# One 512-column moving operand for two groups of tokens in the first product of a retention and MLP kernel

## The chip, the cores and the metric

One core of one Trainium2 chip. The metric is the device time of one execution, in microseconds, as a median of runs. Engines are called as in the profile: PE is TensorE, DVE is VectorE, ACT is ScalarE, POOL is GpSimd, SP is SyncE.

## The reference

Two parts, one behind the other, all in float32 (B 4, H 8, S 768, D 64; 3072 tokens, d_model 512, d_ff 2048):

```python
for t in range(S):                       # retention, for each batch and head
    state = gamma * state + k[t] (outer) v[t]
    y[t] = scale * q[t] @ state
x = y as [3072 tokens, 512]
h = x @ w_in                             # the first product
g = h * erf(softplus(h))                 # the gate
out = g @ w_out                          # the second product
```

`w_in` and `w_out` arrive in 64-bit words and are converted in the kernel.

## The kernel before

**Tiling.** The 3072 tokens are 24 chunks of 128 and 12 groups of 256 (`GT`), two chunks to a group. d_ff is 16 pieces of 128 (`ft`), or 8 pairs of them (`n`). Both products run on operands that are split into rounded rows: each float32 operand becomes `hi`, `lo` and `dif` in float32r, and three matmuls stand for one. `hi` and `lo` products add up in one PSUM bank `a`, `dif` in another, `b`; `together` (lines 284 and 285) puts them together, ScalarE first, VectorE second.

**First stage.** Groups 0 and 1 are done in a prologue with float32 matmuls (line 620) while `w_in` is being converted. From group 2 on there is one period for each group g. It holds eight units; `unit(g, n)` makes two pieces of d_ff for the 256 tokens of g with 24 matmuls of 256 columns (line 645), and its `put` evacuates them into a tile `h` and writes `h` to DRAM (`HID`, line 668, GpSimd's queue). Units take turns at two pairs of PSUM banks; in the last period at four pairs.

Into the periods, in an order written out by hand, go:

- on TensorE, `on_pe`: the retention for the next group's chunks a = 2g+2 and b = 2g+3. `begin` (lines 526 and 533: scores from k and q, then k times v) stands before the unit with index 2, `results` (lines 571 and 582) before the one with index 5;
- on ScalarE and VectorE, `beside`: `states`, `crossed_sums` (line 601) and `split_x` (lines 276 to 278), which makes the next group's split rows `x_hi`, `x_lo`, `x_dif`; `prepare`, which transposes the next k and q (line 505), scales q (line 500) and, at the start of the following period, scales v (line 510); the conversion of `w_out` (`convert`), which ends in a write of float32 rows to DRAM (`WOF`, line 238); splits of weights (lines 268 to 270);
- on SyncE's queue, `load_pair`: 32 small loads of k and q (line 144), two of v (line 133), two of k (line 155) for the chunks after next;
- on GpSimd's queue, `load_quarter`: the loads of `w_out` (line 187), one in each unit of the first period and then in units 2 to 5.

The order of the program is kept on each engine. Tiles of 4 KB for each partition come from one pool of 39 slots (`big`), of 8 KB from a pool of 4 (`wide`: `w_in` and `w_out` as they arrive, later the first split pieces of `w_out`). A slot is handed on when the last access to its tile is over, and the first writer of the new tile waits for that.

**Second stage.** For each group and quarter of d_ff, a load of 512 KB from `HID` (line 763), softplus (768), erf (772), product (782), split (276 to 278), and 24 matmuls of 512 columns (line 827). The first groups' gates and the splits of `w_out` are begun in the last two periods of the first stage.

Of the kernel before, what the change touches and what calls it, by code (L numbers as in the profile page):

```python
# [21 lines left out]
P = 128  # L22
# [27 lines left out]
def kernel(  # L50
# [21 lines left out]
    n_ft = d_ff // P  # L72
    NPC = n_ft // 2
    DH = d_model // 2
    assert D == 64 and d_model == H * D and n_k == HP == 4 and S % GT == 0 and NJ % 2 == 0
    assert H == 8 and n_ft == 16 and NC > JPC and GT == 2 * C

    const = ctx.enter_context(tc.tile_pool(name="const", bufs=1))
    big = ctx.enter_context(tc.tile_pool(name="big", bufs=39))
    small = ctx.enter_context(tc.tile_pool(name="small", bufs=6))  # L80
    wide = ctx.enter_context(tc.tile_pool(name="wide", bufs=4))
    scratch = ctx.enter_context(tc.tile_pool(name="scratch", bufs=1, space=bass.MemoryType.DRAM))
    ps_r = ctx.enter_context(tc.tile_pool(name="ps_r", bufs=2, space=PSUM))
    ps_h = ctx.enter_context(tc.tile_pool(name="ps_h", bufs=2, space=PSUM))
# [10 lines left out]
        return wide.tile([P] + shape, dtype, name=name, tag="b8")  # L95


    HID = [scratch.tile([P, n_ft, GT], F32, name=f"hid{g}") for g in range(NG)]
    WOF = [scratch.tile([P, 2, d_model], F32, name=f"wof{n}") for n in range(NPC)]

    KN, QN, V, KB, QB, KT, QT, SC, AM, SU = {}, {}, {}, {}, {}, {}, {}, {}, {}, {}
# [65 lines left out]
    def load_piece(n, part=None):  # L167

        if n not in RAW:
            RAW[n] = b8("raw", [2 * d_model], I64)  # L170
        f = slice(2 * P) if part is None else slice(part * P, (part + 1) * P)
        each = 1 if part is None else 2
        for g in range(0, n_k, each):
            nc.sync.dma_start(
                RAW[n].rearrange("p (g f) -> p g f", g=n_k)[:, g : g + each, f],
                w_in[g * P : (g + each) * P, n * 2 * P : (n + 1) * 2 * P].rearrange(
                    "(g p) f -> p g f", p=P
                )[:, :, f],
            )
# [13 lines left out]
    def conversion(n):  # L193

        WF[n] = b4("w", [2, 2, 2 * P])
        POWER[n] = b4("power", [2, 2, 2 * P])
        for part in range(2) if n < 4 else (None,):
            f = slice(2 * P) if part is None else slice(part * P, (part + 1) * P)  # L200
            words = RAW[n].bitcast(U32).rearrange("p (h a b w) -> p h a b w", h=2, a=2, w=2)[:, :, :, f]
            to, power = WF[n][..., f], POWER[n][..., f].bitcast(U32)
            number = to.bitcast(U32)
            lo, hi = words[..., 0], words[..., 1]
            nc.vector.tensor_scalar(power, hi, 0x7FF00000, None, op0=ALU.bitwise_and)
            exponent = partial(nc.scalar.activation, power, power, AF.Relu, bias=below, scale=8.0)
            if n < NPC:
                exponent()
            else:
                behind.append(exponent)  # L210
            yield
            nc.vector.tensor_scalar(
                number, hi, 0xFFFFF, 1 << 20, op0=ALU.bitwise_and, op1=ALU.bitwise_or
            )
            if part is None:
                yield
            nc.vector.scalar_tensor_tensor(to, number, 2.0**32, lo, op0=ALU.mult, op1=ALU.add)
            yield
            nc.vector.scalar_tensor_tensor(
                power, hi, 1 << 31, power, op0=ALU.bitwise_and, op1=ALU.bitwise_or  # L220
            )
            if part != 0:
                del RAW[n]
                if n + 4 < NPC:
                    load_piece(n + 4)
                if n < 2:
                    load(JPC + n)
                    load_values(JPC + n)
            if part is None:
                yield  # L230
            nc.vector.scalar_tensor_tensor(
                to, to, 2.0**-52, power.bitcast(F32), op0=ALU.mult, op1=ALU.mult,
            )
            if n < NPC:
                done.update(("in", 2 * n + u) for u in (range(2) if part is None else (part,)))
            yield
        if n >= NPC:
            nc.gpsimd.dma_start(
                WOF[n - NPC], WF.pop(n).rearrange("p h a f -> p (h a f)").rearrange("p (f c) -> p f c", f=2)
            )  # L240

    def weights():

# [359 lines left out]
    def split_x(j):  # L603
        g, i = divmod(j, 2)
        if i == 0:
            X[g] = [b4(f"x_{x}", [HP, GT], F32R) for x in ("hi", "lo", "dif")]
        at = slice(i * C, (i + 1) * C)
        split(X[g], (slice(None), slice(None), at), XC[g][:, :, at])

# [25 lines left out]
    def unit(g, n):  # L635
# [26 lines left out]
        def put():  # L662
# [3 lines left out]
            else:  # L666
                together(h, a, b)
            nc.gpsimd.dma_start(HID[g][:, 2 * n : 2 * n + 2], h)  # L668

        return put  # L670

# [86 lines left out]
    def load_hidden(n):  # L758
# [1 line left out]
        if n >= NG * NU:  # L760
            return
        HID_[n] = b4("hid", [4, GT])
        nc.sync.dma_start(HID_[n], HID[n // NU][:, n % NU * 4 : n % NU * 4 + 4])

    def softplus(k):
        for n in (2 * k, 2 * k + 1) if k < NH else ():
# [26 lines left out]
        nc.sync.dma_start(WO[n], WOF[n])  # L793

    first_w = []

    def split_w_out(n):
        to = None
        if n < 2:
            if n == 0:  # L800
                first_w.extend(b8(f"w_{x}", [2, 2 * d_model], F32R) for x in ("hi", "lo", "dif"))
            to = [x[:, n] for x in first_w]
        if n == 2:
            x = b8("w_2", [2, 2 * d_model], F32R)
            to = [x[:, 0], x[:, 1], b4("w_dif", [2 * d_model], F32R)]
        split_weights(n, WO.pop(n), to, W_OUT)

    Y = {}
# [35 lines left out]
        for n in (2 * k, 2 * k + 1):  # L844
            load_hidden(n)

    def on_pe(g):

        a, b = 2 * g + 2, 2 * g + 3
        if a >= NJ:  # L850
            return {}
        if g < NG - 2:
            m = 3 if g == G2 else 2
            return {
                m: [(begin, a, ps_h), (begin, b, ps_r)],
                5: [(results, a, None, ps_h), (results, b, None, ps_r)],
            }
        return {1: [(begin, a)], 2: [(results, a)], 3: [(begin, b)], 5: [(results, b)]}

    def beside(g, prep, next_prep):  # L860

        a, b = 2 * g + 2, 2 * g + 3
        if g == G2:
            return {
                1: [(split_weights, 4)],
                2: [(split_weights, 5)],
                3: [(states, a), (states, b)],
# [1 line left out]
                5: [(crossed_sums, a), (split_x, a)],  # L869
                6: [(crossed_sums, b), (split_x, b)],  # L870
                7: [(steps, next_prep, 3)],
            }
        if g == G2 + 1:
            return {
                0: [(steps, prep)],
                1: [(split_weights, 7)],
                2: [(states, a)],
                3: [(states, b)],
                5: [(crossed_sums, a), (split_x, a)],
                6: [(crossed_sums, b), (split_x, b)],  # L880
                7: [(steps, next_prep, 3)],
            }
        if g < NG - 2:
            return {
                0: [(steps, prep)] + [(convert, 1)] * (g < NG - 3),
                1: [(convert, 2)],
                2: [(states, a), (convert, 1)],
                3: [(states, b), (convert, 1)],
                4: [(convert, 2)],
                5: [(crossed_sums, a), (split_x, a)],  # L890
                6: [(crossed_sums, b), (split_x, b)],
                7: [(steps, next_prep, 3)],
            }
        if g == NG - 2:
            return {
                0: [(steps, prep), (load_w_out, 0)],
                1: [(states, a), (load_w_out, 1)],
                2: [(crossed_sums, a), (split_w_out, 0), (load_hiddens, 0)],
                3: [(states, b), (split_x, a)],
                4: [(split_w_out, 1), (softplus, 0)],  # L900
                5: [(erf, 0), (crossed_sums, b), (load_w_out, 2)],
                6: [(split_x, b), (gated, 0), (load_hiddens, 1)],
                7: [(split_w_out, 2), (split_g, 0)],
            }
        return {
            0: [(split_g, 1), (softplus, 1), (load_w_out, 3)],
            1: [(erf, 1), (load_w_out, 4)],
            2: [(split_w_out, 3), (load_w_out, 5)],
            3: [(gated, 1), (split_w_out, 4)],
            4: [(split_g, 2), (load_w_out, 6), (load_hiddens, 2)],  # L910
            5: [(split_w_out, 5), (load_w_out, 7)],
            6: [(split_g, 3)],
            7: [(split_w_out, 6)],
        }

    for g in range(G2, NG):
        pair = load_pair(2 * g + 4) if 2 * g + 4 < NJ else iter(())
        next_prep = prepare(2 * g + 4) if 2 * g + 4 < NJ else iter(())
        pe, other = on_pe(g), beside(g, prep, next_prep)
        for i, n in enumerate((0, 7, 1, 2, 3, 4, 5, 6) if g == G2 else range(NPC)):  # L920
            for f, *args in pe.get(i, ()):
                f(*args)
            put = unit(g, n)
            steps(pair, 3)
            for part in itertools.islice(quarters, int(g == G2 or 2 <= i < 6)):
                load_quarter(part)
            if g == NG - 1:
                W.pop(n)
            for f, *args in other.get(i, ()):
                f(*args)  # L930
            put()
# [69 lines left out]
```

## Time and profile before

| | |
|---|---|
| median of 3 runs | 625.7 us (625.42 to 626.14) |
| the profiled execution | 626.08 us, span 624.4 us, granted clock 0.999 |
| TensorE busy | 616.4 us, 99% of the span |
| VectorE, ScalarE, GpSimd busy | 473.1, 346.7, 100.7 us |
| matmuls of line 645 (first product from group 2 on) | 1896, all of 256 columns |
| matmuls of line 827 (second product) | 1152, all of 512 columns |
| DMA | 106.37 MB, 164178 packets |
| first stage | until about 358 us of the span, one period 27.2 to 27.5 us |

The page counts an engine as busy from the start of an instruction to its end; TensorE's matmuls overlap, so for a stream of them the distance between starts counts, which its timeline shows. In the profile's lines `a <-b` behind an idle time names what ended it.

### The profile page before, as it was taken

How to read it: one execution, taken by the hardware profiler on the slowest of the kernel's cores; microseconds unless marked ns; L12 is line 12 of the kernel's file. 1: busy time of each engine (PE TensorE's matmuls, PEld its weight loads, DVE VectorE, ACT ScalarE, POOL GpSimd, SP SyncE). 2: the span in 40 equal slices, each digit the busy share in tenths (PEclk: the TensorE clock that was granted, in tenths of full speed). 3: DMA queues.
4: the chain of work that ended last, by engine and by line, in shares of the span. 5: the costliest groups of instructions: out<-in, count | busy, mean ns of one | idle time of the engine just before them, and what ended most of it. 6: DMA issues, size and time to landing. Idle time of an engine off the chain costs nothing.

```text
span 624.4 us, 14691 instructions
## 1 busy us (share of the span) xinstructions
PE 616.4 (99%) x6078; PEld 554.8 (89%) x6078; DVE 473.1 (76%) x608; ACT 346.7 (56%) x430; POOL 100.7 (16%) x192
## 2 busy tenths in 40 slices
PE   8999999999999999999999999999999999999997
PEld 7888899999999999999999978888888888888885
DVE  6898897859598796987767997867686776768640
ACT  3433443232323424232369779898889889888920
POOL 1075332222231422222111110000000000000000
PEclk9999999999999999999999999999999999999999
DMA  9998778787669799796945752353425314432300
GB/s 204 320 243 272 160 164 230 188 212 168 190 188 233 200 245 259 191 231 171 292 159 174 245 186 63 106 170 111 123 103 169 134 63 140 151 103 85 102 34 34
DMA packets 164178, 106.37 MB, mean 170 GB/s; under 512 B 139920, under 2 KB 141200, under 8 KB 164112
## 3 DMA queue, kind: packets, MB, share of 16 engines
q1 hardware_dynamic: 151264, 67.53, 42.3%
q0 software_dynamic: 12288, 37.77, 17.4%
q8 instruction: 47, 0.77, 0.5%
q10 hardware_dynamic: 560, 0.14, 0.1%
q14 instruction: 19, 0.16, 0.1%
HBM read 69.75 MB, written 35.65 MB: 169 GB/s over the span
## 4 chain that ended last, share of the span: by engine, by line
PE 96%; DMA 1%; DVE 1%; SPq 1%; issue 0%; ACT 0%; DVEq 0%
PE o L645 35%; PE o L827 21%; PE hp L827 10%; PE r L827 10%; PE hp L620 9%; PE hp L526 1%; PE hp L645 1%; PE r L645 1%; DMA q<-in_q_dram 1%; PE r L571 1%; PE r L526 1%; PE hp L533 1%; PE r L582 1%; PE r L533 1%; PE hp L571 1%; PE hp L582 1%
## 5 line engine op out<-in xcount | busy, mean ns | idle before, releaser
L645 PE MATMUL o<-x_hi,w_hi 128*128 128x256 f32 x600 | 149.6, 287 | 0.0
L645 PE MATMUL o<-x_lo,w_lo 128*128 128x256 f32 x600 | 147.1, 283 | 0.0
L645 PEld LDWEIGHTS o<-x_hi,w_hi 128*128 128x128 f32 x600 | 114.9, 192 | 1.4
L645 PEld LDWEIGHTS o<-x_lo,w_lo 128*128 128x128 f32 x600 | 115.1, 192 | 0.1
L284 ACT ACTIVATE h<-o 128x512 f32<-128x512 f32 x75 | 44.6, 596 | 125.9 <-PE o L645 125.1
L782 DVE TENSOR_TENSOR e<-hid,e 128x1024 f32<-128x1024 f32 x48 | 56.6, 1221 | 58.3 <-ACT e L772 58.3
L645 PE MATMUL o<-x_dif,w_dif 128*128 128x256 f32 x600 | 84.2, 283 | 0.5 <-DVE h L285 0.5
L668 POOL DMA_DIRECT2D hid<-h x80 | 44.6, 558 | 207.2 <-DVE h L285 204.6
L645 PEld LDWEIGHTS o<-x_dif,w_dif 128*128 128x128 f32 x600 | 77.4, 192 | 0.7 <-DVE h L285 0.7
L827 PE MATMUL o<-w_dif,g_dif 128*128 128x512 f32 x192 | 73.7, 389 | 0.0
L285 DVE SCALAR_TENSOR_TENSOR h<-o,h 128x512 f32<-128x512 f32 x75 | 51.2, 682 | 25.4 <-ACT h L284 13.1
L827 PE MATMUL o<-w_hi,g_hi 128*128 128x512 f32 x168 | 65.4, 389 | 0.0
L827 PE MATMUL o<-w_lo,g_lo 128*128 128x512 f32 x168 | 65.4, 389 | 0.0
L278 DVE SCALAR_TENSOR_TENSOR g_dif<-g_hi,g_lo 128x1024 fp32r<-128x1024 f32 x48 | 58.8, 1225 | 3.2
L276 ACT ACTIVATE g_hi<-e 128x1024 fp32r<-128x1024 f32 x48 | 51.0, 1063 | 18.1 <-DVE e L782 15.6
L277 DVE TENSOR_TENSOR g_lo<-e,g_hi 128x1024 fp32r<-128x1024 f32 x48 | 58.6, 1221 | 0.2
L620 PE MATMUL hp<-xT,w 128*128 128x256 f32 x256 | 56.9, 381 | 0.0
L620 PEld LDWEIGHTS hp<-xT,w 128*128 128x128 f32 x256 | 48.1, 190 | 6.6
L768 ACT ACTIVATE e<-hid 128x1024 f32<-128x1024 f32 x48 | 48.2, 1052 | 0.3
L772 ACT ACTIVATE e<-e 128x1024 f32<-128x1024 f32 x48 | 48.2, 1052 | 0.3
L827 PEld LDWEIGHTS o<-w_dif,g_dif 128*128 128x128 f32 x192 | 36.0, 188 | 7.4
L827 PE MATMUL hp<-w_dif,g_dif 128*128 128x512 f32 x96 | 37.5, 390 | 0.6 <-DVE h L285 0.6
(168 smaller groups left out, 1068.3 us busy)
## 6 DMA issues: line engine op xcount, KB each, us to landing
hid<-hid SPq DMA_DIRECT2D x48, 512.0 KB, 4.8
hid<-h POOLq DMA_DIRECT2D x80, 256.0 KB, 3.6
raw<-in_moe_w_in_dram SPq DMA_DIRECT2D x32, 256.0 KB, 5.9
raw<-in_moe_w_out_dram POOLq DMA_DIRECT2D x32, 256.0 KB, 5.1
v<-in_v_dram SPq DMA_DIRECT2D x24, 256.0 KB, 5.5
out_dram<-y SPq DMA_DIRECT2D x23, 256.0 KB, 2.1
kb<-in_k_dram SPq DMA_DIRECT2D x144, 32.0 KB, 2.8
qb<-in_q_dram SPq DMA_DIRECT2D x144, 32.0 KB, 2.8
```

The costliest lines, as they stand in the source:

```text
L276: nc.scalar.activation(hi, x, AF.Copy, scale=KEEP)
L277: nc.vector.tensor_tensor(lo, x, hi.bitcast(F32), op=ALU.subtract)
L278: nc.vector.scalar_tensor_tensor(dif, hi.bitcast(F32), Z, lo.bitcast(F32), op0=ALU.mult, op1=ALU.subtract)
L284: nc.scalar.activation(to, a, AF.Copy, scale=1 + 1 / Z)
L285: nc.vector.scalar_tensor_tensor(to, b, -1 / Z, to, op0=ALU.mult, op1=ALU.add)
L620: nc.tensor.matmul(HP_[ft][:, g], w[:, kk, ft % 2 * P : (ft % 2 + 1) * P], XC[g][:, kk], start=(kk == 0), stop=(kk == n_k - 1),)
L645: nc.tensor.matmul(to[:, u], W[n][i][:, kk * 2 * P + u * P : kk * 2 * P + (u + 1) * P], X[g][i][:, kk], start=(u == 0 and kk == 0 and i == ...
L668: nc.gpsimd.dma_start(HID[g][:, 2 * n : 2 * n + 2], h)
L768: nc.scalar.activation(E[n], HID_[n], AF.Softplus)
L772: nc.scalar.activation(E[n], E[n], AF.Erf)
L782: nc.vector.tensor_tensor(E[n], HID_.pop(n), E[n], op=ALU.mult)
L827: nc.tensor.matmul(Y[g][t][x // 2], G[n][x][:, f, t * P : (t + 1) * P], W_OUT[ft // 2][x][:, ft % 2 * d_model : (ft % 2 + 1) * d_model], s ...
```

## The change

The first product takes two groups at once. `pair_unit(g, ft)` makes one piece of d_ff (128 columns of `w_in`) for the 512 tokens of groups g and g+1: 12 matmuls, whose moving operand is two runs of 256 columns, one from each group. So half of d_ff is done for groups (g, g+1) in one period and the other half for (g+1, g+2) in the next. Period 3 keeps five single units, period 4 has six pair units and one single unit, periods 5 to 11 have eight pair units each, and a new period 12 has the last four single units of group 11.

The split rows live in three tiles of three groups each (`XR`, a ring) outside of `big`; the ring's space is that of five slots of `big` and two of `wide`, and holds two pieces of `w_in` before and three split pieces of `w_out` after it is a ring. From period 4 to 11 `h` holds one piece for two groups; it is written as a whole to `HID2`, and the second stage reads it back in runs of 1 KB instead of 4 KB; in period 4 it is written in two halves to `HID`. `on_pe` and `beside` become `period`, with `begin` before index 1 and `results` before index 3 in period 3, 1 and 4 in period 4, 2 and 5 in periods 5 to 9. The loads of `w_out` and the last periods' work on the gates and on `w_out` are placed anew. The write to `WOF` is issued with the last step of a conversion, not with the first of the next.

```diff
+    FIRST = 4
-    big = ctx.enter_context(tc.tile_pool(name="big", bufs=39))
+    big = ctx.enter_context(tc.tile_pool(name="big", bufs=34))
-    wide = ctx.enter_context(tc.tile_pool(name="wide", bufs=4))
+    wide = ctx.enter_context(tc.tile_pool(name="wide", bufs=2))
+    ring = ctx.enter_context(tc.tile_pool(name="ring", bufs=1))
...
     def split_x(j):
         g, i = divmod(j, 2)
         if i == 0:
-            X[g] = [b4(f"x_{x}", [HP, GT], F32R) for x in ("hi", "lo", "dif")]
+            if g == JPC // 2:
+                X[g] = [b4(f"x_{x}", [HP, GT], F32R) for x in ("hi", "lo", "dif")]
+            else:
+                if not XR:
+                    XR.extend(
+                        ring.tile([P, 3, HP, GT], F32R, name=f"x_{x}", tag=f"x{i}")
+                        for i, x in enumerate(("hi", "lo", "dif"))
+                    )
+                X[g] = [x[:, g % 3] for x in XR]
...
+    def place_of(g, of):
+
+        return int(of % 3 > min(g % 3, (g + 1) % 3))
+
+    def pair_unit(g, ft):
+
+        pool = next(last_turn) if g == NG - 2 else ps_o
+        own = next(turn) if pool is ps_o else None
+        names = [f"o{2 * own + i}" if pool is ps_o else "hp" if pool is ps_h else "r" for i in range(2)]
+        a, b = (pool.tile([P, 2, GT], F32, name=name) for name in names)
+        n, u = divmod(ft, 2)
+        at = sorted((g % 3, (g + 1) % 3))
+        at = slice(at[0], at[1] + 1, at[1] - at[0])
+        for to, parts in ((a, (0, 1)), (b, (2,))):
+            for kk, i in itertools.product(range(n_k), parts):
+                nc.tensor.matmul(
+                    to,
+                    W[n][i][:, kk * 2 * P + u * P : kk * 2 * P + (u + 1) * P],
+                    XR[i][:, at, kk],
+                    start=(kk == 0 and i == parts[0]),
+                    stop=(kk == n_k - 1 and i == parts[-1]),
+                )
+
+        def put():
+            h = b2("h", [2, GT])
+            together(h, a, b)
+            if g < FIRST:
+                for of in (g, g + 1):
+                    nc.gpsimd.dma_start(HID[of][:, ft], h[:, place_of(g, of)])
+            else:
+                nc.gpsimd.dma_start(HID2[g][:, ft % 8], h)
+
+        return put
...
+        g, i = divmod(n, NU)
+        of = g if g % 2 == i // 2 else g - 1
+        if FIRST <= of < NG - 1:
+            src = HID2[of][:, i % 2 * 4 : i % 2 * 4 + 4, place_of(of, g)]
+        else:
+            src = HID[g][:, i * 4 : i * 4 + 4]
+        nc.sync.dma_start(HID_[n], src)
...
+        if g == G2 + 1:
+            units = [one(g, n) for n in range(5)]
+            return units, joined(1, 3, g), {
+                0: [(steps, prep)],
+                1: [(states, a), (states, b)],
+                2: [(split_weights, 7)],
+                3: [(crossed_sums, a), (split_x, a), (crossed_sums, b), (split_x, b)],
+                4: [(steps, next_prep, 3)],
+            }, ()
+        if g == G2 + 2:
+            units = [two(g - 1, ft) for ft in range(10, n_ft)] + [one(g, 4)]
+            return units, joined(1, 4, g), {
...
+        if g < NG:
+            units = [two(g - 1, ft) for ft in range(8 * (g % 2 == 0), 8 * (g % 2 == 0) + 8)]
+        if g < NG - 2:
+            return units, joined(2, 5, g), {
+                0: [(steps, prep), (convert, 1)],
+                1: [(convert, 2)],
+                2: [(states, a), (convert, 1)],
+                3: [(states, b), (convert, 1)],
+                4: [(convert, 1 if g in (6, 9) else 2)],
                 5: [(crossed_sums, a), (split_x, a)],
                 6: [(crossed_sums, b), (split_x, b)],
                 7: [(steps, next_prep, 3)],
+            }, {5: (2, 3, 4, 5), 6: (1, 2, 3, 4, 5, 6, 7), 7: (0, 4, 5, 6, 7), 8: (2, 3, 4, 5)}.get(g, ())
...
+        return [one(NG - 1, n) for n in range(4, NPC)], {}, {
+            0: [(split_w_out, 5), (load_w_out, 6)],
+            1: [(split_g, 3), (load_w_out, 7)],
+            2: [(split_w_out, 6)],
+        }, ()
```

More of the change, by code (lines that the diff above doesn't have):

```diff
@@ L95, in b8 @@
         return wide.tile([P] + shape, dtype, name=name, tag="b8")
-    HID = [scratch.tile([P, n_ft, GT], F32, name=f"hid{g}") for g in range(NG)]
+    HID = {g: scratch.tile([P, n_ft, GT], F32, name=f"hid{g}") for g in (*range(FIRST + 1), NG - 1)}
+    HID2 = {
+        g: scratch.tile([P, n_ft // 2, 2, GT], F32, name=f"hids{g}") for g in range(FIRST, NG - 1)
+    }
+    XR = []
     WOF = [scratch.tile([P, 2, d_model], F32, name=f"wof{n}") for n in range(NPC)]
@@ L169, in load_piece @@
         if n not in RAW:
-            RAW[n] = b8("raw", [2 * d_model], I64)
+            if n % 4 < 2:
+                RAW[n] = b8("raw", [2 * d_model], I64)
+            else:
+                raw = ring.tile([P, 3 * d_model], I64, name="raw", tag=f"x{n % 4 - 2}")
+                RAW[n] = raw[:, : 2 * d_model]
         f = slice(2 * P) if part is None else slice(part * P, (part + 1) * P)
@@ L235, in conversion @@
                 done.update(("in", 2 * n + u) for u in (range(2) if part is None else (part,)))
+            else:
+                nc.gpsimd.dma_start(
+                    WOF[n - NPC],
+                    WF.pop(n).rearrange("p h a f -> p (h a f)").rearrange("p (f c) -> p f c", f=2),
+                )
             yield
[L237 to L240, printed above, removed]
     def weights():
@@ L668, in put @@
             nc.gpsimd.dma_start(HID[g][:, 2 * n : 2 * n + 2], h)
+        return put
[17 more added lines that the diff above has]
+                    stop=(kk == n_k - 1 and i == parts[-1]),
+                )
+        def put():
[4 more added lines that the diff above has]
+                    nc.gpsimd.dma_start(HID[of][:, ft], h[:, place_of(g, of)])
+            else:
+                nc.gpsimd.dma_start(HID2[g][:, ft % 8], h)
         return put
@@ L762, in load_hidden @@
         HID_[n] = b4("hid", [4, GT])
-        nc.sync.dma_start(HID_[n], HID[n // NU][:, n % NU * 4 : n % NU * 4 + 4])
+        g, i = divmod(n, NU)
+        of = g if g % 2 == i // 2 else g - 1
+        if FIRST <= of < NG - 1:
+            src = HID2[of][:, i % 2 * 4 : i % 2 * 4 + 4, place_of(of, g)]
+        else:
+            src = HID[g][:, i * 4 : i * 4 + 4]
+        nc.sync.dma_start(HID_[n], src)
     def softplus(k):
@@ L795 @@
     first_w = []
+    IN_RING = {2: 0, 6: 1, 7: 2}
     def split_w_out(n):
@@ L800, in split_w_out @@
             if n == 0:
[L801 to L805, printed above, removed]
+                first_w.extend(b8(f"w_{x}", [2, 2 * d_model], F32R) for x in ("hi", "lo"))
+            to = [x[:, n] for x in first_w] + [b4("w_dif", [2 * d_model], F32R)]
+        if n in IN_RING:
+            to = [x[:, IN_RING[n]].rearrange("p k t -> p (k t)") for x in XR]
         split_weights(n, WO.pop(n), to, W_OUT)
@@ L845, in load_hiddens, with joined, period @@
             load_hidden(n)
-    def on_pe(g):
+    def joined(at, to, g):
         a, b = 2 * g + 2, 2 * g + 3
[L850 to L860, printed above, removed]
+        return {
+            at: [(begin, a, ps_h), (begin, b, ps_r)],
+            to: [(results, a, None, ps_h), (results, b, None, ps_r)],
+        }
+    def period(g, prep, next_prep):
         a, b = 2 * g + 2, 2 * g + 3
+        one, two = partial(partial, unit), partial(partial, pair_unit)
         if g == G2:
-            return {
+            units = [one(g, n) for n in (0, 7, 1, 2, 3, 4, 5, 6)]
+            return units, joined(3, 5, g), {
                 1: [(split_weights, 4)],
@@ L871, in beside @@
                 7: [(steps, next_prep, 3)],
-            }
+            }, range(8)
         if g == G2 + 1:
-            return {
+            units = [one(g, n) for n in range(5)]
+            return units, joined(1, 3, g), {
                 0: [(steps, prep)],
-                1: [(split_weights, 7)],
-                2: [(states, a)],
-                3: [(states, b)],
+                1: [(states, a), (states, b)],
[7 more added lines that the diff above has]
+                0: [(steps, prep), (convert, 1)],
+                1: [(states, a), (convert, 1)],
+                2: [(states, b), (convert, 1)],
+                3: [(convert, 2)],
+                4: [(crossed_sums, a), (split_x, a), (convert, 1)],
+                5: [(crossed_sums, b), (split_x, b)],
+                6: [(convert, 1), (steps, next_prep, 3)],
+            }, (4, 5, 6, 6)
+        if g < NG:
+            units = [two(g - 1, ft) for ft in range(8 * (g % 2 == 0), 8 * (g % 2 == 0) + 8)]
+        if g < NG - 2:
+            return units, joined(2, 5, g), {
+                0: [(steps, prep), (convert, 1)],
+                1: [(convert, 2)],
+                2: [(states, a), (convert, 1)],
+                3: [(states, b), (convert, 1)],
+                4: [(convert, 1 if g in (6, 9) else 2)],
                 5: [(crossed_sums, a), (split_x, a)],
@@ L881, in beside @@
                 7: [(steps, next_prep, 3)],
[L882 to L893, printed above, removed]
+            }, {5: (2, 3, 4, 5), 6: (1, 2, 3, 4, 5, 6, 7), 7: (0, 4, 5, 6, 7), 8: (2, 3, 4, 5)}.get(g, ())
@@ L894, in beside @@
         if g == NG - 2:
-            return {
+            return units, {1: [(begin, a)], 2: [(results, a)], 3: [(begin, b)], 5: [(results, b)]}, {
                 0: [(steps, prep), (load_w_out, 0)],
                 1: [(states, a), (load_w_out, 1)],
-                2: [(crossed_sums, a), (split_w_out, 0), (load_hiddens, 0)],
+                2: [(crossed_sums, a), (split_w_out, 0)],
                 3: [(states, b), (split_x, a)],
[L900 to L916, printed above, removed]
+                4: [(split_w_out, 1), (load_hiddens, 0)],
@@ new lines, in period @@
+                5: [(crossed_sums, b)],
+                6: [(split_x, b), (softplus, 0), (load_w_out, 2)],
+                7: [(erf, 0), (gated, 0)],
+            }, ()
+        if g == NG - 1:
+            return units, {}, {
+                0: [(split_g, 0), (split_w_out, 2), (load_w_out, 3)],
+                1: [(split_g, 1), (load_hiddens, 1)],
+                2: [(split_w_out, 3)],
+                3: [(softplus, 1), (load_w_out, 4)],
+                4: [(erf, 1)],
+                5: [(split_w_out, 4), (load_w_out, 5)],
+                6: [(gated, 1)],
+                7: [(split_g, 2), (load_hiddens, 2)],
+            }, ()
@@ L917 @@
+        return [one(NG - 1, n) for n in range(4, NPC)], {}, {
+            0: [(split_w_out, 5), (load_w_out, 6)],
+            1: [(split_g, 3), (load_w_out, 7)],
+            2: [(split_w_out, 6)],
+        }, ()
+    for g in range(G2, NG + 1):
         pair = load_pair(2 * g + 4) if 2 * g + 4 < NJ else iter(())
         next_prep = prepare(2 * g + 4) if 2 * g + 4 < NJ else iter(())
-        pe, other = on_pe(g), beside(g, prep, next_prep)
-        for i, n in enumerate((0, 7, 1, 2, 3, 4, 5, 6) if g == G2 else range(NPC)):
+        units, pe, other, loads = period(g, prep, next_prep)
+        for i, work in enumerate(units):
@@ L921 @@
             for f, *args in pe.get(i, ()):
                 f(*args)
-            put = unit(g, n)
+            put = work()
             steps(pair, 3)
-            for part in itertools.islice(quarters, int(g == G2 or 2 <= i < 6)):
+            for part in itertools.islice(quarters, loads.count(i) if g > G2 else 1):
                 load_quarter(part)
-            if g == NG - 1:
-                W.pop(n)
+            if g == NG - 1 and i % 2:
+                W.pop(i // 2)
+            if g == NG:
+                W.pop(NPC - 4 + i)
```

## The prediction

> **What bounds the kernel now.** The page first: its engine line and its chain of work.
>
> ```profile
> PE 616.4 (99%) x6078; PEld 554.8 (89%) x6078; DVE 473.1 (76%) x608; ACT 346.7 (56%) x430; POOL 100.7 (16%) x192
> ...
> PE 96%; DMA 1%; DVE 1%; SPq 1%; issue 0%; ACT 0%; DVEq 0%
> ```
>
> TensorE is 96% of the chain, so time is won only where TensorE needs less, and lost only where something newly makes it wait. I call the eight units of one g in the loop a period. Busy time does not tell what a matmul costs, because matmuls overlap; the distance of their starts does. From TensorE's timeline, first product, then second:
>
> ```profile
> 301.47 0.28 PE L645 MATMUL o<-x_hi,w_hi 128*128 128x256 f32 x1
> 301.59 0.28 PE L645 MATMUL o<-x_lo,w_lo 128*128 128x256 f32 x1
> 301.71 0.28 PE L645 MATMUL o<-x_hi,w_hi 128*128 128x256 f32 x1
> ...
> 550.81 0.39 PE L827 MATMUL r<-w_hi,g_hi 128*128 128x512 f32 x1
> 551.04 0.39 PE L827 MATMUL r<-w_lo,g_lo 128*128 128x512 f32 x1
> 551.27 0.39 PE L827 MATMUL r<-w_dif,g_dif 128*128 128x512 f32 x1
> ```
>
> A 256-column matmul takes 120 ns of the stream. A 512-column one takes 226.7 ns: the chain gives 21.76 us for 96. If cost is a + b x columns, b is 106.7/256 = 0.417 ns, and each matmul carries 13.3 ns that do not depend on its columns. That is what a wider operand saves once.
>
> Next, what lies close behind TensorE: VectorE's timeline in period 6 (197.1 to 224.6), where the retention's second part ended on TensorE at 215.85.
>
> ```profile
> 215.71 0.48 DVE L601 TENSOR_TENSOR xT<-xT,hp 128x128 f32<-128x128 f32 x2 [1.03 <-ACT xT L590]
> 217.18 0.69 DVE L277 TENSOR_TENSOR x_lo<-xT,x_hi 128x512 fp32r<-128x512 f32 x1 [0.98 <-ACT x_hi L276]
> 217.90 0.69 DVE L278 SCALAR_TENSOR_TENSOR x_dif<-x_hi,x_lo 128x512 fp32r<-128x512 f32 x1
> ...
> 222.86 1.23 DVE L505 STREAM_TRANSPOSE kT<-kb 128x1024 f32<-128x1024 f32 x1
> 224.02 1.18 DVE L500 TENSOR_TENSOR qb<-qb,kq_b 128x1024 f32<-128x1024 f32 x1
> 225.23 1.25 DVE L505 STREAM_TRANSPOSE qT<-qb 128x1024 f32<-128x1024 f32 x1
> 226.40 0.65 DVE L285 SCALAR_TENSOR_TENSOR h<-o,h 128x512 f32<-128x512 f32 x1
> 226.98 1.21 DVE L510 TENSOR_TENSOR v<-v,kq_s 128x1024 f32<-128x1024 f32 x1
> ```
>
> VectorE enters each period 2 to 3 us late, with transposes and the scaling of v that the next "begin" needs. Now that is hidden: "begin" stands two units (5.76 us) into the period. SyncE's timeline and the stages' table show the third neighbour, the loads of k, q and v:
>
> ```profile
> 191.25 4.34 SPq L155 DMA_DIRECT2D kn<-in_k_dram  x2
> 195.70 1.01 SPq L144 DMA_DIRECT2D kb<-in_k_dram  x1
> ...
> 224.60:252.00 27.40, 27.40 (x434) 27.00 (x433) 22.19 (x35) 8.28 (x15) 7.34 (x13) 1.00 0.90 233
> ```
>
> From 168 us on SyncE issues one pair's loads right behind the other's, 25 to 27.5 us each, with the DMA engines 77 to 90% busy (next to last column).
>
> **The change, part by part.** All against the profiled execution: 626.08 us, span 624.4, 1.7 us around it; the median is 0.4 lower.
>
> *Wide operand.* Pair units: 6 in period 4, 8 in each of periods 5 to 11, 62 in all. Each runs 12 matmuls of 512 columns in place of 24 of 256: 12 x 226.7 = 2.72 us for 2.88. Saved: 62 x 12 x 13.3 ns = 9.9 us, all of it on the chain. The trace shows no matmul whose moving operand is two pieces of 256, as here; bounds are no gain (each piece pays 13.3) and 9.9. I take 9.9: the 13.3 ns follows the instruction in both rows.
>
> The Trainium skill, "TensorE: Matmul & The Clock Gate", Back-to-back issue gap, has columns over 2.4 GHz plus about 2.5 ns. By it the saving is only 744 x 2.5 ns = 1.9 us, an estimate; the rows with their 13.3 ns disagree with it.
>
> *Shorter lead of "begin".* Period 3 keeps only five units, and periods 3 and 4 have "begin" one unit after their start instead of two.
> - Period 4, the worst place. In period 3 both chunks' sums and splits now stand in one unit, then unit 4 with the transposes, then period 4's scaling of v. Let t = 0 be the end of "results". VectorE by the rows above: sums and split of a until 2.7 (215.71 to 218.59), of b another 2.65 until 5.4, evacuation 0.6, transposes 3.6 until 9.6, evacuation 0.6, scaling of v 1.2 until 11.4. TensorE: two units (5.76) and one pair unit (2.72), so "begin" is wanted at 8.5. It waits for qT until 9.6, 1.1 us; its scores take 0.5 (120.04 to 120.56 in the timeline), then its second half waits for v from 10.1 to 11.4, 1.3. Sum 2.4 us. Who else waits: the evacuations behind these on VectorE; the unit after "begin" needs the bank evacuated at 10.2, so it does not.
> - Period 3: v is scaled until 117.8; "begin" reaches its second half at 114.2 + 2.88 + 0.5 = 117.6. 0.2 us.
> - Period 10, "begin" at one unit before and after: it waits 0.2 us for v now; a unit shorter by 0.16 and a VectorE later by 0.3 make it some 0.4 more.
> Together +3.0 us; bounds 0 (if VectorE runs ahead) and 5.
>
> *Split rows in a ring.* No extra instruction. It removes one wait: in period 4 a row's last split takes a slot that a weight's write to DRAM still holds.
>
> ```profile
> 165.97 0.69 DVE L278 SCALAR_TENSOR_TENSOR x_dif<-x_hi,x_lo 128x512 fp32r<-128x512 f32 x1 [3.56 <-DMA wof<-w]
> ```
>
> That made VectorE late enough that TensorE lost 0.77 us at 173.8 to 174.6. Gone with the ring, and that write is now issued a step earlier: -0.8. The price is 34 slots where there were 39; I count the pool just full in periods 4 to 9, and the slots that SyncE's loads get have been free for some units, so I cost this at nothing. Without that cover a load comes late (a rival).
>
> *Evacuations.* One put per unit as before, ScalarE 0.60 and VectorE 0.68 us. VectorE has 21 to 25 us of work in a period (the stages' table); 27.4 becomes 26.1, so it is at most 96% full, with a bank pair to spare. Nothing, as long as VectorE is in time by one unit. GpSimd's queue gets six more writes (period 4 writes two halves; 0.56 us each, queue 16% busy): nothing.
>
> *Order at the end.* Four units of group 11 move behind the pair units, and the work on w_out and the gates is spread over twelve units where it had eight. Before, TensorE lost 0.85 us at 359 where the second product waited for VectorE's last evacuations. VectorE still has some 22.5 us of work in period 11's 21.8; I take half back: -0.4 (bounds -0.85 and +1).
>
> *Reads of hid.* Groups 4 to 11 are read in pieces of 1 KB instead of 4 KB. Loads land 3 to 4 us ahead of their softplus in most cases of the second stage (448.84 issued, 453.87 landed, used 457.22); up to 1.5 us longer stays hidden. Nothing.
>
> *Loads of k, q, v.* They start earlier than before (now SyncE stands idle from 156.8 to 168.2 until x_hi's slot is free, a wait the ring removes), but the two short periods want them 11.5 us earlier and later periods are 1.3 us shorter. Taking each stream as long as before, they lead their first use by 1.5 to 4 us in periods 5 to 10: no stall. A denser DMA load may stretch them; I add 0.4, bounds 0 and 6.
>
> Sum: 626.1 - 9.9 + 3.0 - 0.8 - 0.4 + 0.4 = 618.4 profiled, 618.0 as a median.
>
> **Rivals.**
> - *The loads set the pace.* If the streams (mean 26.3 us) grow by 5% to 27.6, each of five periods lacks 1.5 us; the lead of about 2 goes first, 5.5 us are lost: 623.5. For it: 0.90 DMA share in period 7, and seven quarters of w_out in period 6 instead of four. Against it: every stream landed 3 us or more before its use.
> - *The ring is one tile (slower).* If the framework orders a write to one third of the ring against reads of the others, each split waits for the running unit and the next unit for the split. Price: 216.50 to 218.59, 2.1 us, for two splits in each of periods 4 to 10: 14 x 2.1 = 29 us, 647. It decides as soon as tiles are tracked whole. Against it: at 215.97 ScalarE writes its columns of xT while VectorE, from 215.71 to 216.19, adds to other columns of the same tile.
> - *The wide operand does not do what it says.* If two pieces pay 13.3 ns each, 9.9 us are missing: 628. If the part that is saved were 2.5 ns and not 13.3, 8.0 are missing: 626, no change; against both stand the two rows, which are 13.3 above 0.417 ns a column alike. The second is what the Trainium skill's "TensorE: Matmul & The Clock Gate" would make of it.
>
> **How the numbers follow.** Forecast 0.66 (615 to 621), paced loads 0.20 (620 to 624.4), ring as one tile 0.05, wide operand without gain 0.05 and with the small gain 0.02, other mishaps 0.02. From the first two, 0.86, I take the range 615.0 to 623.8, which leaves their ends and all else out, under 0.2. Below 615 all new waits would have to be hidden. The measurement can tell 0.2%, 1.25 us: faster 0.86, same 0.03, slower 0.11.
>
> **What would show it.** Right: L645's successor at 226.7 ns between starts; some 744 fewer matmuls and weight loads; periods 5 to 9 of 26.1 us; one gap of 2 to 3 us about 136 us in front of and inside "begin", no 3.6 us wait of x_dif. Wrong: starts over 235 ns; "begin" waiting for a load of k or v in periods 6 to 10; pair units waiting for splits; evacuations that release a unit late in several periods.

## The result, and the profile after

The changed kernel takes 618.6 us (median of its three undisturbed runs, 618.34 to 619.43; the kernel before beside them 625.8): ratio 0.9888, 95% interval 0.9869 to 0.9908. In a second set of runs it took 618.96 us, ratio 0.9895 (0.988 to 0.991). Forecast were 618.0 us and a range of 615.0 to 623.8. In one further execution, the first one that was profiled, TensorE ran at half its rate from start to end (1233.9 us; 445 ns between the starts of 512-column matmuls), with no record of the granted clock in its trace and for a cause that stays open; all that follows is read from an execution at the full rate, with a span of 617.1 us.

The page of the changed kernel, engines and chain:

```profile
PE 608.0 (99%) x5334; PEld 515.3 (84%) x5334; DVE 472.9 (77%) x608; ACT 347.1 (56%) x430; POOL 104.1 (17%) x198
...
PE 93%; SPq 3%; DVE 2%; DMA 1%; issue 1%; ACT 0%; DVEq 0%
```

744 matmuls and as many weight loads are gone (6078 to 5334), VectorE has the same 608 instructions. TensorE is still nearly the whole chain. Its timeline in period 4 shows both what was won and what it cost (L707 is the new matmul, L538 and L545 are `begin`, formerly 526 and 533):

```profile
135.06 0.39 PE L707 MATMUL o<-x_hi,w_hi 128*128 128x512 f32 x1
135.29 0.39 PE L707 MATMUL o<-x_lo,w_lo 128*128 128x512 f32 x1
135.51 1.07 PE L707 MATMUL o<-x_dif,w_dif 128*128 128x512 f32 x4
137.31 0.69 PE L538 MATMUL hp<-qT,kT 64*64 64x64 f32 x32 [0.73 <-DVE qT L517]
139.02 0.69 PE L545 MATMUL hp<-v,kn 64*64 64x64 f32 x32 [1.01 <-DVE v L522]
139.53 0.65 PE L538 MATMUL r<-qT,kT 64*64 64x64 f32 x32
```

The 512-column matmuls with two runs of 256 follow each other at 227 ns, like those of the second product. `begin` waits twice, first for qT, then for v. VectorE at the same time:

```profile
132.43 0.69 DVE L290 SCALAR_TENSOR_TENSOR x_dif<-x_hi,x_lo 128x512 fp32r<-128x512 f32 x1
133.04 0.68 DVE L297 SCALAR_TENSOR_TENSOR h<-o,h 128x512 f32<-128x512 f32 x1
133.64 1.24 DVE L517 STREAM_TRANSPOSE kT<-kb 128x1024 f32<-128x1024 f32 x1
134.79 1.18 DVE L512 TENSOR_TENSOR qb<-qb,kq_b 128x1024 f32<-128x1024 f32 x1
136.01 1.25 DVE L517 STREAM_TRANSPOSE qT<-qb 128x1024 f32<-128x1024 f32 x1
137.18 0.65 DVE L297 SCALAR_TENSOR_TENSOR h<-o,h 128x512 f32<-128x512 f32 x1
137.76 1.20 DVE L522 TENSOR_TENSOR v<-v,kq_s 128x1024 f32<-128x1024 f32 x1
```

It works without a gap from the splits to the scaling of v; qT ends at 137.26 and `begin` starts at 137.31, v ends at 138.96 and the second half starts at 139.02. All waits of TensorE in this execution are these:

```profile
PE hp L545 <- DVE v L522: 1.5, 2, 1.0
PE o L391 <- POOL ident masks.py:199: 1.5, 1, 1.5
PE r L439 <- ACT kqT L433: 0.9, 2, 0.6
PE hp L538 <- DVE qT L517: 0.7, 1, 0.7
```

The second and third line belong to the prologue and stand in the kernel before too. The wait for VectorE's last evacuation at the start of the second product (0.6 us, 0.85 with what it brings) is not there any more, and no wait for a load or for a split.

### The profile page after: what moved, and what is told of

Its sections match the earlier page's. It is cut to its first block, busy times and chain, and to the rows that moved or that the text cites. A ratio compares the mean times of both kernels' runs of the same rounds, so it can differ in the third digit from the quotient of the medians.

```text
span 1232.1 us, 13251 instructions
## 1 busy us (share of the span) xinstructions
PE 1226.1 (100%) x5334; PEld 844.6 (69%) x5334; DVE 482.4 (39%) x608; ACT 347.7 (28%) x430; POOL 102.2 (8%) x198
## 4 chain that ended last, share of the span: by engine, by line
PE 99%; DMA 0%; DVE 0%; DVEq 0%; issue 0%
PE o L707 27%; PE o L887 22%; PE hp L887 11%; PE r L887 11%; PE hp L640 10%; PE o L665 7%; PE hp L707 1%; PE r L707 1%; PE hp L538 1%; PE r L538 1%; PE r L583 1%; PE r L594 1%; PE hp L545 1%; PE r L545 1%; PE r L439 1%; PE o L478 1%
## 5 line engine op out<-in xcount | busy, mean ns | idle before, releaser
L707 PE MATMUL o<-x_hi,w_hi 128*128 128x512 f32 x232 | 158.4, 683 | 0.0
L707 PE MATMUL o<-x_lo,w_lo 128*128 128x512 f32 x232 | 155.4, 670 | 0.0
L640 PE MATMUL hp<-xT,w 128*128 128x256 f32 x256 | 120.8, 680 | 0.0
L707 PE MATMUL o<-x_dif,w_dif 128*128 128x512 f32 x232 | 118.8, 675 | 0.0
L707 PEld LDWEIGHTS o<-x_hi,w_hi 128*128 128x128 f32 x232 | 70.9, 306 | 39.2 <-issue 37.0
L707 PEld LDWEIGHTS o<-x_dif,w_dif 128*128 128x128 f32 x232 | 68.4, 295 | 41.7 <-issue 37.7
L707 PEld LDWEIGHTS o<-x_lo,w_lo 128*128 128x128 f32 x232 | 67.5, 291 | 30.3 <-issue 26.1
L722 POOL DMA_DIRECT2D hids<-h x56 | 31.7, 566 | 304.3 <-DVE h L297 304.3
L665 PE MATMUL o<-x_hi,w_hi 128*128 128x256 f32 x120 | 52.6, 452 | 0.0
L665 PE MATMUL o<-x_lo,w_lo 128*128 128x256 f32 x120 | 51.2, 437 | 0.0
L887 PEld LDWEIGHTS o<-w_lo,g_lo 128*128 128x128 f32 x120 | 36.0, 300 | 20.3 <-issue 18.5
```

What stands on the lines that cost most here:

```text
L640: nc.tensor.matmul(HP_[ft][:, g], w[:, kk, ft % 2 * P : (ft % 2 + 1) * P], XC[g][:, kk], start=(kk == 0), stop=(kk == n_k - 1),)
L665: nc.tensor.matmul(to[:, u], W[n][i][:, kk * 2 * P + u * P : kk * 2 * P + (u + 1) * P], X[g][i][:, kk], start=(u == 0 and kk == 0 and i == ...
L707: nc.tensor.matmul(to, W[n][i][:, kk * 2 * P + u * P : kk * 2 * P + (u + 1) * P], XR[i][:, at, kk], start=(kk == 0 and i == parts[0]), sto ...
L722: nc.gpsimd.dma_start(HID2[g][:, ft % 8], h)
L887: nc.tensor.matmul(Y[g][t][x // 2], G[n][x][:, f, t * P : (t + 1) * P], W_OUT[ft // 2][x][:, ft % 2 * d_model : (ft % 2 + 1) * d_model], s ...
```

## The experiments

All were compared with the kernel before on the same chip.

**The same kernel again.**

> The changed kernel once more, for a profile at TensorE's full rate. My theory: 7 to 8 us below the kernel before; between two starts of L707's matmuls 226.7 ns; one wait of 2.4 us in and ahead of 'begin' of period 4 (for qT, then for v), 0.2 us in period 3 and some 0.6 in period 10; no wait of x_dif for a weight's write; the loads of k and v land 1.5 to 4 us ahead of their use. The rival of paced loads: waits of TensorE for loads in several of the periods 5 to 10 that add up to more than 1 us.

Measured 618.96 us; the lines above are its profile. In period 4 `begin` starts 0.80 us later than its place in the stream asks (1.12 us behind the start of the matmul before it, where 0.32 is the rule), its second half another 1.19 later; in period 3 the second half is 0.18 late, in period 10 0.65, where it was 0.17 before. No wait of TensorE for a load. In the lead of the loads the expectation was wrong in part, see the last experiment.

**The wide operand taken back.** Each matmul of a pair unit becomes two, one for each group:

```diff
-            for kk, i in itertools.product(range(n_k), parts):
-                nc.tensor.matmul(to, W[n][i][...], XR[i][:, at, kk], ...)
+            for s, slot in enumerate(sorted((g % 3, (g + 1) % 3))):
+                for kk, i in itertools.product(range(n_k), parts):
+                    nc.tensor.matmul(to[:, s], W[n][i][...], XR[i][:, slot, kk], ...)
```

> The changed kernel, but each 512-column matmul of a pair unit is two of 256, one for each group; all else as it is. Theory (13.3 ns for each matmul, whatever its columns): 744 matmuls more, 9.9 us slower than the changed kernel, less 0.2 us that the longer units give 'begin'; 2 us slower than the kernel before. Rival (a fixed part of 2.5 ns): 1.9 us slower than the changed kernel. Rival (the gain came from the ring and the new order of work): the same time as the changed kernel.

629.19 us, ratio 1.005 (1.0036 to 1.0064): 10.2 us above the changed kernel and slower than the one before. So none of the gain comes from ring, order and placement; all of it is the operand's. Without it 3.4 us are lost, but 2.2 of them are one gap that only this run shows, so they are not the price of the new order alone. The stream of the first product, summed from the distances of starts in the loop without the waits, is 237.9 to 238.0 us in two traces of the kernel before, 237.8 here and 228.6 in the changed kernel: 9.2 us between the last two, 12.4 ns for each of the 744 matmuls. The rest of the difference between the two profiled executions (10.3 us) is that gap, where TensorE waited for nothing that the profile shows, less 0.6 us of shorter waits of `begin` and 0.4 us of a shorter prologue:

```profile
PE o L708 <- issue: 2.1, 1, 2.1
```

**`begin` of period 4 one unit later.**

```diff
-            return units, joined(1, 4, g), {
+            return units, joined(2, 4, g), {
...
-                1: [(states, a), (convert, 1)],
-                2: [(states, b), (convert, 1)],
+                1: [(convert, 1)],
+                2: [(states, a), (states, b), (convert, 1)],
```

> The changed kernel with 'begin' of period 4 one unit later, before the third unit; its states go with it. Theory (2.4 us are lost in period 4 because 'begin' comes before qT and v are ready): the wait is gone, 2.0 to 2.5 us faster than the changed kernel. Rival (VectorE's lateness is only passed on to the evacuations or to the next 'results'): less than 0.5 us faster, with a new wait at 'results' of the same period.

617.16 us, ratio 0.9861 (0.9848 to 0.9875), 1.8 us faster than the changed kernel beside it, a little under the 2.0 to 2.5 us expected. In its trace `begin` of period 4 runs through, and `results` has no new wait:

```profile
140.00 0.69 PE L538 MATMUL hp<-qT,kT 64*64 64x64 f32 x32
140.52 0.65 PE L545 MATMUL hp<-v,kn 64*64 64x64 f32 x32
140.99 0.65 PE L538 MATMUL r<-qT,kT 64*64 64x64 f32 x32
```

So the lost time was the order's: `begin` came too early for VectorE, whose work is the same, and nothing was passed on.

**The early write alone.** The kernel before, with the write of a converted weight issued in the last step of its conversion:

```diff
             if n < NPC:
                 done.update(...)
+            else:
+                nc.gpsimd.dma_start(WOF[n - NPC], WF.pop(n)...)
             yield
-        if n >= NPC:
-            nc.gpsimd.dma_start(WOF[n - NPC], WF.pop(n)...)
```

> The kernel before with one line of the change alone: the write of a converted weight to DRAM is issued with the last step of its conversion. Theory (TensorE lost 0.77 us near 174 us because x_dif waited 3.6 us for a slot that this write held): the write starts some 3 us earlier, the wait shrinks to below 1 us, and 0.8 us are won. Rival (the write is slow because the DMA engines are full, and its start matters little; only another slot for the rows helps): no change, and the wait stays over 2 us.

626.07 us in 11 runs, ratio 1.0005 (0.9997 to 1.0014): no gain. Yet the wait of x_dif is gone from its trace. The wait went as the theory had it, and the gain stayed away as the rival had it; neither explains both. A second profile of the kernel before does.

> The kernel before, once more, for a second profile. If the 3.6 us wait of x_dif for the weight's write near 166 us, and the 0.77 us that TensorE lost at 174, belong to the kernel, they are here again. If they belong to one execution (the write landed late by chance), the wait is another length or absent; then the 0.8 us that the prediction took for it was not there to win in most runs, as the run with the write issued early, which was no faster, suggests.

625.36 us, span 623.6. The wait is there, but shorter:

```profile
165.18 0.69 DVE L278 SCALAR_TENSOR_TENSOR x_dif<-x_hi,x_lo 128x512 fp32r<-128x512 f32 x1 [2.75 <-DMA wof<-w]
```

and TensorE loses nothing behind it. At 3.56 us VectorE released the bank 0.7 us too late, at 2.75 just in time. This is the whole difference between the two profiled executions of the kernel before, 0.7 us: the first stage, from its first unit to the second product, took 271.95 and 271.18 us.

**Both repairs.** The later `begin`, and for periods 3 and 10 the scaling of v at the end of the period before:

```diff
-                7: [(steps, next_prep, 3)],          # period 2
+                7: [(steps, next_prep, 4)],
...
-                7: [(steps, next_prep, 3)],          # periods 5 to 9
+                7: [(steps, next_prep, 4 if g == NG - 3 else 3)],
```

> The changed kernel with 'begin' of period 4 one unit later, and with the scaling of v for periods 3 and 10 put at the end of the period before, ahead of the last evacuation instead of behind it. Theory (what is left of TensorE's waits in the first stage is 0.13 us in period 3 and 0.5 to 0.7 us in period 10, both for the scaled v): 0.5 us faster than with the later 'begin' alone, 2.3 us faster than the changed kernel. Rival (the second half of 'begin' in period 10 waits for the load of k, which lands at the same time): no faster than with the later 'begin' alone.

616.14 us with the kernel before at 625.31, ratio 0.9853 (0.9839 to 0.9868), the fastest of all. Against the ratio with the later `begin` alone that is 0.5 us, inside both intervals; the traces decide: in period 10 `begin` now starts its halves at 290.86 and 291.42, and no wait of TensorE is left between the prologue and the end.

```profile
290.86 0.69 PE L538 MATMUL hp<-qT,kT 64*64 64x64 f32 x32
291.42 0.69 PE L545 MATMUL hp<-v,kn 64*64 64x64 f32 x32
```

**More loads.**

```diff
             for to, src in ((KB[j], k), (QB[j], q)):
                 for u in range(HP):
                     nc.sync.dma_start(...)
+                nc.sync.dma_start(more[part, ...], ...)   # 32 KB, not read by anybody
                 yield
```

> The changed kernel with 8 more loads of 32 KB on SyncE's queue for each pair of chunks (40 for 32), copies of k and q into a DRAM tile that nobody reads. In the profile of the changed kernel the last of k and q lands 0 to 4 us ahead of its transpose in periods 6 to 9 and k for 'begin' 0.2 to 2 us ahead in periods 9 and 10. Theory (the loads are off the path, but by less than one period's gain): some 4 us more of SyncE's queue for each pair; the lead is used up within two periods and four or five periods become 2 to 4 us longer, 8 to 15 us in all. Rival (the loads have the lead of 1.5 to 4 us that the prediction gave them and catch up while SyncE idles): less than 4 us slower.

651.56 us, ratio 1.0411 (1.0386 to 1.0435): 33 us above the changed kernel, far over what either theory gave. A load that is added takes 0.56 us of SyncE's queue, 4.5 us for each pair, and with eight pairs inside the loop 36 us. Periods 4 to 9 now measure 28 to 34 us. That the loss comes so near to 36 us is chance: matmul by matmul against the trace of the changed kernel, the first stage is 34.8 us longer, 24.8 us of it in eleven new or longer waits, 9.6 us in matmuls at half rate behind such waits (see the last section) and 0.4 us elsewhere. In the stretch from 220 to 240 us VectorE waits for a load, its evacuation comes late, and TensorE with it:

```profile
DVE kT L524 <- DMA kb<-in_k_dram: 6.6, 1, 6.6
...
PE o L714 <- DVE h L304: 5.5, 1, 5.5
```

So the loads have too little lead to take 4.5 us more in each period. The trace of the changed kernel shows how little. SyncE's queue around the start of period 8 (the pair's last loads, then the next pair's first):

```profile
233.37 3.37 SPq L162 DMA_DIRECT2D kn<-in_k_dram  x2
236.84 3.62 SPq L151 DMA_DIRECT2D kb<-in_k_dram  x4
```

And VectorE's first use of the pair:

```profile
236.72 1.23 DVE L517 STREAM_TRANSPOSE kT<-kb 128x1024 f32<-128x1024 f32 x1
```

Of this pair's small loads the last of k landed at 232.71, 4.0 us before this transpose, and the last of q at 236.35, 1.5 us before q is scaled (237.88); of the next pair's at 262.25 and 262.92, 0.5 and 1.0 us before the same uses. The shortest lead of these loads, from period 5 to 10, is 9.3, 5.8, 3.2, 1.5, 0.5 and 3.5 us. In the kernel with both repairs it comes down to 0.1 us, in period 7, and TensorE still waits for none. The table of stretches, one for each of periods 5 to 7, shows how full the DMA engines are (stretch and length; busy time and instructions of PE, PEld, DVE, ACT and POOL; the granted clock, the busy share of the DMA engines, and GB/s):

```profile
159.50:185.60 26.10, 26.10 (x339) 21.59 (x338) 23.55 (x37) 8.22 (x15) 8.12 (x16) 1.00 0.94 238
185.60:211.80 26.20, 26.20 (x353) 21.76 (x352) 21.80 (x35) 8.34 (x15) 9.65 (x17) 1.00 0.92 247
211.80:238.10 26.30, 26.30 (x337) 21.81 (x337) 21.66 (x35) 9.26 (x16) 8.62 (x15) 1.00 0.90 227
```

The DMA engines are 90 to 94% busy in these periods of 26.1 to 26.3 us, and one pair's loads follow the other's without a pause: the three pairs that start between 181.6 and 236.8 us take 27.3, 27.9 and 27.4 us to the next pair's first load, a little more than a period. That the full DMA engines set this length was not tested.

## Why the prediction was right, and which terms were mis-sized

- **Wide operand, -9.9 us: right.** Measured -9.3 (237.9 in the second profile of the kernel before, 228.6 here). The 13.3 ns belong to the instruction also when its operand is two runs. The missing 0.6 us is a restart, about 0.03 us each time: in each of the 18 pair units behind the retention or behind a single unit, some five starts lie 228 to 236 ns apart before 227 is reached, and behind the retention the first distance is 335 to 339 ns. The figure of the Trainium skill's "TensorE: Matmul & The Clock Gate", Back-to-back issue gap, 2.5 ns a matmul, would have given 1.9 us, an estimate; the run with the narrow operand decides for 12.4 ns.
- **Shorter lead of `begin`, +3.0 us: right, mechanism and place.** Period 4: 2.0 instead of 2.4; period 3: 0.2 as forecast; period 10: 0.5 more than before, instead of 0.4. Together 2.7, of which the two repairs brought back 1.8 and about 0.5.
- **Wait of x_dif, -0.8 us: wrong step.** It was taken from one execution in which the write landed late. The second profile shows the wait without a loss, and the early write alone wins nothing. A term that stands or falls with the landing of one transfer should have been taken at half, or looked for in the spread of the runs: 0.8 us is as much as they differ.
- **Order at the end, -0.4 us: too small.** The whole 0.85 us at the start of the second product are gone, in the changed kernel and in the two repaired ones. The half that was taken back for VectorE's full period 11 was not needed.
- **Evacuations, reads of hid, slots: nothing, right.** No evacuation released a bank late, the second stage has its old spacing (226.7 ns), and no load waited long enough for a slot to be seen at TensorE.
- **Loads of k, q and v, +0.4 us: no wait was measured, and the lead was read wrongly.** Forecast was a lead of 1.5 to 4 us in periods 5 to 10; it began at 9.3 us and fell to 0.5 us in period 9. The step that failed is the length of a pair's stream against the shorter period. Streams that run without a pause take 27.3 to 27.9 us, about as long as in the first trace of the kernel before (27.5, 27.6, 27.8 and 25.0), but more than the mean of 26.3 that the rival of paced loads started from and more than a period of 26.1 to 26.3. So the streams were as long as that rival asked (27.6); its 5.5 us did not come because the lead began at 9 us and not at 2. That the lead lasted until the last pair was luck.
- **Ring as one tile: fell.** Pair units and splits overlap in every period.

By the terms as measured, from the second profile of the kernel before: 623.6 - 9.3 + 2.7 - 0.85 = 616.2 of span, against 617.1. Of the rest 0.4 lies in the prologue, which differs as much from run to run, 0.3 behind the last matmul and 0.3 in the retention's own matmuls. Two of the forecast's terms, -0.8 that was not there and -0.4 that should have been twice as much, nearly offset each other; that the forecast of 618.0 us came within 1 us owes something to luck.

## What to carry to other kernels

Count a stream of matmuls by the distance of their starts at two widths: the part that does not depend on the columns is what a wider operand saves, and here one subtraction gave the gain within 0.6 us. When a period gets shorter, ask of each queue that fills a whole period whether it still fits, by its end against its first use and not by its mean load; and move a step that another engine feeds only after counting that engine's chain up to it. A wait that a transfer ends should be looked up in a second profile before it enters the sum.

## What had not been expected of the hardware

- After TensorE has stood for some microseconds, it can restart at half rate: in the run with more loads, 512-column starts are 425 to 428 ns apart instead of 227 behind waits of 5.5 us and of 4.0 and 2.2 us, for up to seven matmuls and the retention's, and the granted clock of the stretch from 200 to 250 us is 0.93. A late load is so paid for beyond its lateness, with 9.6 us in that execution. A wait of 1.7 us in the same run and the gap of the narrow run, in which TensorE was idle for 2.1 us, did not do that; one of 2.2 us did, by the clock's record 0.8 us after its end.
- One gap of 2.2 us of TensorE in the narrow run falls together with the load of 16 KB of instructions, which began at 235.9, as the gap did, 13.4 us after the one before it. No such gap was seen in the changed kernel, with half as many matmuls in a unit, nor in the kernel before, with as many. That the late instructions caused it was not tested.
